# Identity, causal mask and row masks from GpSimd's affine selects in place of a load, and the second pair's output products ahead of the third FFN step

## The chip, the cores and the metric

The kernel runs on one NeuronCore of a Trainium2 chip. The metric is the device time of one execution in microseconds; the engines are TensorE (PE), VectorE (DVE), ScalarE (ACT), GpSimd (POOL) and SyncE (SP, which only issues DMAs here).

## The reference

A chunked state-space layer feeds a feed-forward layer with squared ReLU. Cut to what matters:

```python
# x (4, 8, 768, 32), a (4, 8, 768), B and C (4, 8, 768, 16), chunk 32
for c in range(nc):
    cum = np.cumsum(log_a[chunk], axis=-1)
    L = np.exp(cum[..., :, None] - cum[..., None, :]) * causal
    M = einsum('bhin,bhjn->bhij', Cc, Bc) * L
    y_intra = einsum('bhij,bhjd->bhid', M, xc)
    y_inter = einsum('bhin,bhnd->bhid', Cc, state) * exp(cum)[..., None]
    y[chunk] = y_intra + y_inter
    state = exp(sum(la)) * state + sum_j Bx * exp(cum[-1:] - cum)
t = y.transpose(0, 2, 1, 3).reshape(3072, 256)
h = maximum(t @ w_in, 0)          # w_in (256, 2048)
out = (h * h) @ w_out             # w_out (2048, 256)
```

## The kernel before

The kernel does not use the reference's chunk of 32. It cuts each of the 4 sequences of 768 tokens into 3 pieces of 256, and works on the 12 pairs (batch, piece) one after the other; `PAIRS` is piece-major, so the first four pairs have no state to carry in. A pair's 256 tokens are two halves `u` of 128, and each half is split by token parity `r`, so that 64 pairs of tokens lie on 64 partitions. The causal factor `exp(cum_i - cum_j)` is split into `P_i * (1/P_j)`, with `P` a running product of `a` (`cp_r`, by DVE's scan on line 484): C is multiplied by `P` and x by `1/P` (`Pinv`), and the products of C and B (`mt`, line 227) are then masked with 0 and 1 (`ph_mask`, line 238).

For one pair the stages are these. `ph_load` loads C, B and x on SP's queue; its `gate` argument is an engine that writes one element of each destination with a memset first, so that the load can't be issued before that engine has come so far. `prep_c`, `prep_b`, `prep_x` scale and cast. `ph_tr` (PE and a DVE copy) or, from pair 4 on, `ph_dtr` (a DMA) transpose. `ph_mt` makes `mt`, `ph_mask` makes `mts`; `ph_u` and `ph_s` make the state (`U`, `z`, `S`); `ph_y` makes the pair's output in PSUM. For pairs 1 to 3 `ph_y` does the products inside the half first (`y_intra`, line 314, 32 small matmuls of `xs` and `mts`), then those with the state (line 347, 8 matmuls of `bct` and `S`), and ends with ScalarE's copy `T` (line 366).

The FFN of one pair ("block") is 8 steps `fp`, two slices of 128 of the 2048 hidden units each. `mm1` is 4 matmuls into a PSUM tile `hps` (pool of 2 buffers), followed by ScalarE's ReLU into `hb` (line 381). `square` is DVE's `h2` (line 387). `mm2` is 4 matmuls into the block's output sum (line 405). `finish_block` copies and stores.

Everything stands under a manual schedule: the program order written in the Python code is the order in each engine's queue. The list `steps` gives the order of FFN steps: steps 0 to 3 are the first half of block 0, 4 to 7 that of block 1, 8 to 15 the second halves, then blocks 2 to 11. In step `s` the loop does: `mm1`, some warm-up matmuls in steps 1 and 2, then what `at(s, ...)` put into `todo`, then `square` of the step before, and from step 4 on one `mm2`. So block 0 runs while pair 1 is still being made: `ph_mt(1)` and two masks are in step 0, `ph_u(1)` and the other masks in step 1, and `ph_y(1)` is called ahead of `mm1` of step 3. Step 4 is the first that needs `T[1]`.

The weights come in four chunks each, cast from fp32 to bf16 on the way, on GpSimd's DMA queue (`load_wi`, line 136; `load_wo`, line 141). The first chunk of `w_in` is issued behind a one-element copy `touch` (line 499) that waits for `P_T`; the second behind `prep_x(0)`; two chunks of `w_out` follow, then `prep_x(1)`, then the memsets that gate the loads of pair 2, then the third chunk of `w_in`. The last three chunks wait behind a `touch` of `T[1]` (line 569, `late_loads`).

The constants come in two DMAs on ScalarE's queue: `cb` (bf16: the identity, the causal mask, `own`, which marks the row's block of 32, and `half`, which marks the row's 16 within it) and behind it `cf` (fp32: `pick` and `spread`, from which `sel` is made on line 481). ScalarE copies the identity and `half` out of `cb` as fp32 (lines 479 and 480). `sel` times `cp_r` gives `P_T` (line 496).

## Time and profile before

| What | Value |
|---|---|
| median of 11 runs | 119.97 us (118.44 to 122.27) |
| the profiled execution | 119.81 us |
| its span, from the first to the last instruction | 118.0 us |
| mean granted TensorE clock in it | 0.998 |
| PE busy | 110.4 us, 94% of the span, 1672 matmuls |
| DVE, ACT, POOL busy | 86.0, 76.3, 33.5 us |
| DMA | 13.63 MB, mean 115 GB/s |

The profile is of one execution. Its times count from the start of the span, and line numbers are those of the kernel before. PE is a matmul, PEld its weight load. In the tables "<-" after an idle time names what ended it; "issue" is idle time for which the profile shows no cause. A line of the chain is start, duration, what. A line of the stretch table is the stretch, its length, then busy us and number of instructions of PE, PEld, DVE, ACT and POOL, then the granted clock, the mean busy share of the 16 DMA engines and GB/s. A line of DMA queues is the queue, packets, MB, and the time that they took as a share of 16 engines' time.

### The profile page before, as it was taken

The numbers are of one execution on the slowest core, as the hardware profiler recorded it, in microseconds if no ns is written. First come the engines' busy times: TensorE is split into PE (matmuls) and PEld (weight loads), VectorE is DVE, ScalarE is ACT, GpSimd is POOL, SyncE is SP. The second block draws the span as 40 slices with busy tenths as digits, with TensorE's granted clock in tenths as the row PEclk, the third lists the DMA queues.
The fourth block names the chain that finished last, engine by engine and source line by source line (L and its number), as shares of the span: only waits on it lengthen the run. The fifth ranks groups of instructions, "written<-read, shape, count | busy, mean of one in ns | idle before, by whom it ended". The sixth has DMA issues, their size and how long they took to land.

```text
span 118.0 us, 4065 instructions
## 1 busy us (share of the span) xinstructions
PE 110.4 (94%) x1672; PEld 91.0 (77%) x1672; DVE 86.0 (73%) x204; ACT 76.3 (65%) x146; POOL 33.5 (28%) x69
## 2 busy tenths in 40 slices
PE   6799669999999999999999999999999999999970
PEld 4576448877977788788788887887887887888960
DVE  6479834699889699798698894984966967844530
ACT  4546738848678577586586677576775865867730
POOL 0079408604884350530404432504300000000000
PEclk9999999999999999999999999999999999999999
DMA  3999999999899945907908928549160020100202
GB/s 86 188 172 119 113 192 197 156 182 183 154 221 169 195 56 129 203 10 159 180 24 166 148 77 164 101 123 190 26 158 8 0 89 6 55 34 0 91 3 89
DMA packets 50019, 13.63 MB, mean 115 GB/s; under 512 B 44304, under 2 KB 49104, under 8 KB 50000
## 3 DMA queue, kind: packets, MB, share of 16 engines
q1 hardware_dynamic: 46400, 10.98, 50.6%
q0 software_dynamic: 3200, 2.10, 13.6%
q10 hardware_dynamic: 400, 0.28, 1.0%
q8 instruction: 13, 0.21, 0.8%
q14 instruction: 6, 0.05, 0.1%
HBM read 10.74 MB, written 3.15 MB: 118 GB/s over the span
## 4 chain that ended last, share of the span: by engine, by line
PE 85%; DMA 8%; ACT 1%; issue 1%; POOL 1%; DVE 0%; ACTq 0%; DVEq 0%
PE ops L405 35%; PE hps L377 35%; DMA w_in_b<-in_moe_w_in_dram 5%; PE Y L314 3%; PE mt L227 3%; DMA cf<-const_f 3%; PE Y L343 2%; PE U L256 1%; PE ctpt L496 1%; POOL xs L183 1%; PE ops_r L405 1%; PE ops L421 1%; PE ops_r L421 1%; PE Y L347 1%; ACT T L366 1%
## 5 line engine op out<-in xcount | busy, mean ns | idle before, releaser
L381 ACT ACTIVATE hb<-hps 128x512 bf16<-128x512 f32 x96 | 57.5, 599 | 30.0 <-PE hps L377 28.9
L377 PE MATMUL hps<-T,w_in_b 128*128 128x256 bf16 x384 | 57.6, 273 | 1.0 <-DMA w_in_b<-in_moe_w_in_dram 0.7
L405 PE MATMUL ops<-w_out_b,h 128*128 128x256 bf16 x360 | 55.0, 273 | 0.0
L387 DVE TENSOR_TENSOR h<-hb 128x512 bf16<-128x512 bf16 x96 | 40.7, 445 | 12.4 <-ACT hb L381 12.3
L377 PEld LDWEIGHTS <-w_in_b 128*128 128x128 bf16 x384 | 37.1, 98 | 5.8 <-DMA w_in_b<-in_moe_w_in_dram 1.2
L405 PEld LDWEIGHTS <-h 128*128 128x128 bf16 x376 | 34.5, 98 | 6.3 <-issue 2.0
L238 DVE TENSOR_TENSOR mts<-mt,cb 128x512 bf16<-128x512 f32 x44 | 29.1, 683 | 9.5 <-PE mt L227 9.4
L183 POOL TENSOR_TENSOR xs<-x_nat,Pinv 128x512 bf16<-128x512 f32 x12 | 13.3, 1108 | 10.2 <-DVE z L293 4.1
L152 POOL TENSOR_TENSOR bc<-C_nat,P_sb 128x128 bf16<-128x128 f32 x16 | 6.7, 441 | 23.4 <-DMA C_nat<-in_C_dram 19.3
L300 DVE TENSOR_TENSOR S<-z,Pown 128x256 bf16<-128x256 f32 x16 | 8.2, 514 | 0.5
L475 PE MATMUL dps<-dum 128*128 128x128 bf16 (+1 forms) x58 | 7.1, 274 | 1.1 <-DVE dum L457 1.1
L366 ACT CAST T<-Y 128x512 bf16<-128x512 f32 x11 | 6.4, 586 | 1.0 <-PE Y L347 1.0
L475 PEld LDWEIGHTS <-dum 128*128 128x128 bf16 x58 | 5.0, 116 | 2.5 <-DVE dum L457 1.1
L443 ACT COPY osb<-ops 128x512 f32<-128x512 f32 x11 | 6.4, 581 | 0.2 <-PE ops L405 0.2
L314 PE MATMUL Y<-mts,xs 64*32 64x128 bf16 x384 | 5.2, 219 | 0.7 <-issue 0.7
L227 PE MATMUL mt<-bct 32*64 32x256 bf16 x192 | 5.3, 291 | 0.0
L314 PEld LDWEIGHTS <-xs 64*32 64x32 bf16 x384 | 3.0, 91 | 2.3 <-issue 1.3
L177 POOL CAST bc<-B_nat 128x128 bf16<-128x128 f32 x16 | 4.5, 308 | 0.7 <-DMA B_nat<-in_B_dram 0.5
L227 PEld LDWEIGHTS <-bct 32*64 32x64 bf16 x192 | 1.9, 105 | 2.5 <-issue 1.7
L293 DVE SCALAR_TENSOR_TENSOR z<-z,Ptot,U 128x64 f32<-128x64 f32 x12 | 3.2, 266 | 0.5 <-PE U L256 0.3
L141 POOL DMA_DIRECT2D w_out_b<-in_moe_w_out_dram x4 | 3.1, 775 | 0.3 <-issue 0.3
L136 POOL DMA_DIRECT2D w_in_b<-in_moe_w_in_dram x4 | 3.1, 782 | 0.0
(72 smaller groups left out, 55.1 us busy)
## 6 DMA issues: line engine op xcount, KB each, us to landing
x_nat<-in_x_dram SPq DMA_DIRECT2D x12, 256.0 KB, 4.4
out_dram<-osb SPq DMA_DIRECT2D x7, 256.0 KB, 2.3
C_nat<-in_C_dram SPq DMA_DIRECT2D x12, 128.0 KB, 3.4
B_nat<-in_B_dram SPq DMA_DIRECT2D x12, 128.0 KB, 3.8
w_in_b<-in_moe_w_in_dram POOLq DMA_DIRECT2D x4, 256.0 KB, 6.2
w_out_b<-in_moe_w_out_dram POOLq DMA_DIRECT2D x4, 256.0 KB, 7.3
out_dram<-osb SPq DMA_DIRECT2D x8, 128.0 KB, 1.8
bct<-bc SPq DMA_TRANSPOSE x8, 4.3
```

The lines of the kernel that those rows point to most:

```text
L152: eng.tensor_tensor(out=_fap(bc[k % 3], r * 384 + 128, [[144, 2], [32, 4], [1, 16]]), in0=_fap(loaded[k]["C"], r * 16, [[128, 2], [32, 4], ...
L183: eng.tensor_tensor(out=_fap(xs, 0, [[256, 2], [32, 8], [1, 32]]), in0=_fap(loaded[k]["x"], 0, [[32, 2], [64, 8], [1, 32]]), in1=_fap(Pinv ...
L227: nc.tensor.matmul(mt[q // 2][64 * u:64 * u + 64, q % 2, r, :, :], bct[32 * q:32 * q + 32, r, 0, u * 64:u * 64 + 64], _fap(bct[32 * q:32 * ...
L238: nc.vector.tensor_tensor(out=v["mts"][:, q], in0=v["mt"][q // 2][:, q % 2] if src is None else src, in1=_fap(cb, 128, [[128, 2], [0, 2], ...
L300: nc.vector.tensor_tensor(out=S_n.rearrange("p (g q d) -> p g q d", g=2, q=4), in0=_fap(z, 0, [[32, 2], [0, 4], [1, 32]]), in1=_fap(Pown, ...
L314: nc.tensor.matmul(Y[u][32 * q:32 * q + 32, g, :], v["xs"][64 * u:64 * u + 64, r, h * 32:h * 32 + 32], v["mts"][64 * u:64 * u + 64, q, r, ...
L366: nc.scalar.copy(out=_fap(T[k], 0, [[64, 2], [128, 4], [1, 64]]), in_=_fap(Y[0], 0, [[512, 2], [64, 4], [1, 64]]))
L377: nc.tensor.matmul(hps[:, i, :], w_in_b[:, g, f * 128:(f + 1) * 128], T[blk][:, g].rearrange("p r u t -> p (r u t)"), start=(g == 0), stop ...
L381: nc.scalar.activation(out=hb, in_=hps, func=AF.Relu)
L387: nc.vector.tensor_tensor(out=h2, in0=hb, in1=hb, op=ALU.mult)
L405: nc.tensor.matmul(o[c], h2[:, i, r * 128:(r + 1) * 128], w_out_b[:, f, c * 128:(c + 1) * 128] if len(o) > 1 else w_out_b[:, f, :], start= ...
L475: nc.tensor.matmul(idle[-1][:, 0:cols], dum[:, 0:128], dum[:, 0:cols], start=True, stop=True, skip_group_check=True)
```

## The change

The DMA of `cb` is gone. `cb` is now made on the chip: DVE fills a tile `ones`, and GpSimd's `affine_select` keeps a one where an affine expression of partition and column fulfils a condition and writes zero elsewhere. The first makes the identity in fp32 (`eye_f`), from which ScalarE now copies the bf16 one (`eye_b`), the other way round than before. Two make an 8-wide `hq`, which DVE reduces to `half`. Two make the causal mask, one for each half of the partitions, and two make `own`. `cf` is loaded as before, and is now the first on ScalarE's queue.

Two things move in the order of work. `ph_y(1)` is called ahead of `mm1` of step 2 in place of step 3. The loads of pair 2, with their three gating memsets on GpSimd, move from ahead of step 0 into step 2, behind a one-element copy that waits for the last mask of pair 1 (`mts[:, 2]`).

```diff
-    cb = const.tile([128, 390], BF16, name="cb")
+    cb = const.tile([128, 388], BF16, name="cb")
...
+    ones = const.tile([128, 256], FP32, name="ones")
+    hq = const.tile([128, 2, 4], FP32, name="hq")
...
         nc.sync.dma_start(out=a_nat, in_=_dap(a, 0, [[256, 96], [1, 256]]))
-        nc.scalar.dma_start(out=cb, in_=cb_d.ap())
         nc.scalar.dma_start(out=cf, in_=cf_d.ap())
...
         nc.vector.memset(dum, 0.0)
+        nc.vector.memset(ones, 1.0)
+
+        def where(out, src, pattern, cm, base, op):
+            nc.gpsimd.affine_select(out=out, in_=src, pattern=pattern, compare_op=op, fill=0.0,
+                                    base=base, channel_multiplier=cm)
+
+        where(eye_f, ones[:, 0:128], [[-1, 128]], 1, 0, ALU.is_equal)
+        where(hq, ones[:, 0:8].rearrange("p (g q) -> p g q", g=2), [[-16, 2], [-32, 4]], 1, 0, ALU.is_ge)
+        where(hq, hq, [[16, 2], [32, 4]], -1, 15, ALU.is_ge)
+        for u in range(2):
+            where(_fap(cb[64 * u:64 * u + 64], 128, [[128, 2], [64, 2], [1, 64]]),
+                  _fap(ones[64 * u:64 * u + 64], 0, [[128, 2], [64, 2], [1, 64]]),
+                  [[-1, 2], [1, 2], [2, 64]], -2, 0, ALU.is_ge)
+        where(cb[:, 384:388], ones[:, 0:4], [[-32, 4]], 1, 0, ALU.is_ge)
+        where(cb[:, 384:388], cb[:, 384:388], [[32, 4]], -1, 31, ALU.is_ge)
         nc.vector.memset(zer, 0.0)
...
-        nc.scalar.copy(out=eye_f, in_=eye_b)
-        nc.scalar.copy(out=half, in_=cb[:, 388:390])
+        nc.scalar.copy(out=eye_b, in_=eye_f)
+        nc.vector.tensor_reduce(out=half, in_=hq, op=ALU.add, axis=mybir.AxisListType.X)
...
         recip(2, 2, 0)
-        ph_load(2, gate=nc.gpsimd)
         idle_tile()
...
         at(0, load_wi, 8, 12)
+
+        def third_loads():
+            nc.gpsimd.tensor_copy(out=touch, in_=live[1]["mts"][:, 2, 0, 0, 0:1])
+            ph_load(2, gate=nc.gpsimd)
+
+        at(2, third_loads)
...
         for s in range(len(steps) + LAG):
-            if s == 3:
+            if s == 2:
                 ph_y(1)
             if s < len(steps):
                 mm1(*steps[s])
```

## The prediction

> **What bounds the kernel now.** I read the page first, then the chain that ended last in its first 19 us, then the DMA queues by stretch, and last a table of instruction counts by stretch.

> ```profile
> PE   6799669999999999999999999999999999999970
> DMA  3999999999899945907908928549160020100202
> ```

> These are the page's slices of 2.95 us. TensorE is full from the seventh slice to the end; only the first six, about 18 us, have holes, and there DMA is full. From 18.36 us on no PE wait is listed. So whatever the change does to the head moves the end one for one, unless it opens a hole later. The chain in that head (start, us, what):

> ```profile
> 1.12 3.02 DMA cf<-const_f
> 4.15 0.02 issue
> 4.17 0.41 ACT sel L481
> ...
> 4.67 1.20 PE ctpt L496 x4
> ...
> 7.56 1.01 POOL xs L183
> 8.57 6.39 DMA w_in_b<-in_moe_w_in_dram
> ...
> 15.01 0.61 PE hps L377 x4
> ...
> 15.78 0.34 PE Y L314 x29
> 16.12 0.66 issue
> 16.78 0.23 PE Y L314 x3
> ...
> 17.29 0.59 ACT T L366
> ```

> Three things to see. The start hangs on cf (4.15) and on a_nat (a_cl at 3.77). The third FFN step waits for the second chunk of w_in_b (14.96). And in the middle of the second pair's output products PE stops for 0.66 us with nothing to wait for: 29 of 32 matmuls run, then "issue".

> The last one decides this forecast, so I looked for what it is. The page has a queue that carries nothing of the kernel's data, and the stretch table counts PE and PEld instructions:

> ```profile
> q8 instruction: 13, 0.21, 0.8%
> ```
> ```profile
> 10.27:16.50 6.23, 4.56 (x129) 3.09 (x128) 4.63 (x14) 3.46 (x8) 2.80 (x7) 1.00 1.06 127
> 16.50:27.34 10.84, 10.41 (x128) 8.27 (x128) 7.01 (x17) 7.23 (x16) 4.34 (x9) 1.00 1.24 182
> 27.34:36.10 8.76, 8.76 (x130) 7.05 (x127) 8.09 (x17) 6.43 (x13) 6.55 (x13) 1.00 1.11 186
> ```

> ```profile
> q0 software_dynamic: 452, 0.37, 86.2%
> ```
> ```profile
> q0 software_dynamic: 365, 0.19, 131.4%
> q8 instruction: 1, 0.02, 5.7%
> ```

> The first answer is for 10.3 to 14.2 us, the second for 14.2 to 15.3. In neither do SP's loads of the third pair appear, though they were issued at 12.03: they too stood behind GpSimd's weight chunks.

> [...] L183's 1108 ns for 512 elements is 2.2 ns each[...]; no run here shows a select.

> **The change part by part.** Times are of the profiled execution (119.81 us, 118.0 of span).

> *Constants.* Removed: cb's DMA (97.5 KB, landed 3.4), its issue of 0.36 us ahead of cf on ACT's queue, two ACT copies (0.30 and 0.19). cf is issued at 0.74 in place of 1.12 and should land near 3.3 to 3.8. Added on DVE: memset of ones, 256 elements; L462's take 0.79 us for two of 384, so 0.27. It delays the gate of x's first load from 2.42 to 2.69, and x's landing from 6.8 to 7.1; xs starts at 7.56, so 0.2 us of cover is left after the gain below. The small reduce (0.2, by L486's 0.18) stands ahead of a_cl, but DVE would be idle there for 0.89 - 0.27 us. Added on ACT: eye_b's copy (0.30) right behind the table load (ends 2.89), ahead of sel: done at 3.2 if the identity is.

> Added on GpSimd: seven selects from about 1.3 us. By L177 (308 ns for 128 elements) and L499 (189 ns for one) below and L152 (441) and L183 above: identity 0.3 to 0.45, two masks 0.45 to 0.65 each, four small ones 0.2 each: 2.0 to 2.6 us, done by 4.0. GpSimd is idle until 6.39 (wait of 5.9 us for P_T), so I take nothing. The cover ends if they take over 5 us.

> So the start hangs on a_nat. If that still lands at 3.75, the scans end at 4.84 as before, but the first matmuls of L496 run during the second scan: P_T 0.14 sooner. If it lands 0.3 sooner with cb out of the way, 0.42. I take 0.3; the first mm1, the masks and the chunks' issue all follow by that.

> The chunks' data don't follow wholly. Loads of the first two pairs (six of 1024 packets each) keep the DMA engines full to about 9 us, then the first two w_in chunks to 14.2. [...] What is saved is cb's own traffic (about 0.1) and the thin stretch at 10 to 11 us: 0.1 to 0.4, I take 0.25 for the second chunk, and so for the fetch behind it: PE's block is there at 16.78 - 0.25 = 16.53.

> *Order.* The program has the same instructions in PE's queue up to U of the second pair. Before, then come mm1 of step 2 (8 instructions), warm-up (6) and 59 of the products: boundary. After, the 64 of the intra part come first, then 9 of the inter part: the boundary falls with 4 of its 8 matmuls left. So PE reaches it sooner, near 15.0, and stands until 16.53. What follows, counted from the block's arrival a:
> - before: T's copy starts a + 0.51 (17.29), ends a + 1.10; mm1 of step 4 starts a + 1.14 (17.92), its psum slot long free, since step 2's ReLU ran at 15.65.
> - after: T's copy starts about a + 0.42, ends a + 1.01. Step 2's mm1 (0.44) is behind the boundary and runs beside it. Its ReLU is behind T on ACT: a + 1.61. With two hps buffers step 4 needs that slot: a + 1.66.

> So the order costs 0.52 while the fetch sets the time, less 0.25 for the earlier fetch: +0.27. The 0.74 us wait for w_in_b disappears, but is paid again at the boundary.

> *Third pair's loads.* Three memsets and three SP issues move from 11.91 behind the masks (14.72 - 0.3, plus 0.19 for the touch, as L569): C at about 14.75 in place of 12.03. No SP DMA is passed, as none stood between. On GpSimd they come behind the third w_in chunk, and Pown and the touch for the late chunks behind them; neither is late, T being later. In before these loads, issued at 12.03, moved nothing before 15.3 anyway; at 14.75 they stand behind w_out's second chunk, so from about 17.1. Between 18.5 and 20.5 GpSimd's queue is nearly empty (the next chunk is issued at 18.46, about 2 us before its data), and C and B fit there: B at 20.9 to 21.5 (before: 12.49 + 8.4 = 20.9). Its reader:

> ```profile
> 22.55 0.49 ACT L175 CAST Bb<-B_nat 128x128 bf16<-128x128 f32 x2
> ```

> Behind it on ACT stand the ReLUs, for which PE waits. Slack 1.9 us; x (22.1 before) is first used by U at 26.5. I take nothing; the bound is below, in the slower rival.

> Sum: 119.81 + 0.27 = 120.1. The median of 11 runs is 119.97, 0.16 above the profiled execution, so this says no change; a measurement of this kernel can tell about 1%, 1.2 us, from none.

> **Rivals.**
> *The fetch comes in time (30%).* The 6.5 us from 10.27 to 16.78 depend on where the fetch falls among the chunks. Early by 1.5 us, the products end near 15.0 and T near 15.7, step 2's ReLU at 16.35 and step 4 starts at 16.4: 1.5 us under 17.92. About 0.2 is given back, as everything reaches the third pair's B sooner: 118.5. For it: later crossings show no stop. Against: the chunks ahead of it stay.
> *The third pair's B is late (21%), slower.* It decides once B lands 1.9 us later than before, since ACT blocks on Bb and its ReLUs with it. If the landing moves with the issue by all of 2.7 us, the stall is 0.8; if T is early, the late chunks close the gap at 18.5 to 20.5 and x and the fourth pair (whose C is already waited for 4.8 us) follow, another 0.5 or more. 120.1 + 0.8 + 0.5 = 121.4.
> *The selects are slow (7%), slower.* [...] It begins to bite past 6.1 us. [...]

> **How the numbers follow.** Likeliest (42%): 120.1, by itself 119.3 to 121.0 (fetch 0.8 sooner, or not sooner at all with 0.4 of waits for B). From the rivals: faster by over 1% 0.22 (most of the first), slower 0.26 (all of the selects, most of late B, a little of the likeliest), within 1% 0.52. The range 118.4 to 121.4 takes in nearly all of the first rival and half of the second.

> **What would show it.** Right: PE's wait in the inter products (L338) of over 1 us put down to "issue", with the q8 transfer near 14; no wait of hps for w_in_b in step 2; ACT running T before the ReLU of step 2; GpSimd's selects done by 4; P_T copied at 5.5 to 5.8; Bb's cast without a wait. Wrong: no "issue" wait in the products, a DMA wait ahead of Bb or tr of the third pair, or a P_T later than 5.9.

## The result: no gain, about one per cent slower or the same

| | changed | before |
|---|---|---|
| first measurement, median of all executions (us) | 120.41 (119.06 to 123.08, 12) | 120.36 (117.95 to 123.84, 47) |
| ratio | 1.0096 [1.0057, 1.0134] | |
| measured again later, median (us) | 121.15 (119.09 to 124.38, 14) | 120.75 (117.56 to 124.31, 51) |
| ratio | 1.0007 [0.9946, 1.0069] | |
| profiled execution (us) | 121.76, span 120.1 | 119.81, span 118.0 |

Executions of one kernel mostly differ by up to 6%, partly by a stretch of 3.4 or 6.8 us in which TensorE runs at half speed, so the ratios compare only the executions near each kernel's fastest (most of them have no such stretch), and medians of all executions stand beside them.

The forecast was 120.1 us and no change. The time lies inside the range, but the first measurement puts the changed kernel 1% above the one before (the second leaves no difference), and the steps that were to lead to 120.1 were mostly not those that happened. What decided was the part of the change that the title does not name, the later loads of the third pair.

First the page's slices of the changed kernel, 3.0 us each:

```profile
PE   6896799938999999999999999999999999999990
PEclk9999999998699999999999999999999999999999
DMA  3999999999759971862933916909624020020202
```

Before, the last hole of PE lay in the sixth slice. Now the ninth slice has 3 tenths, and behind it the granted clock falls. The chain that ended last, in the first 32 us (start, us, what):

```profile
0.81 2.49 DMA a_nat<-in_a_dram
...
5.97 5.72 DMA w_in_b<-in_moe_w_in_dram
...
12.78 1.95 DVE mts L229 x4
...
15.18 0.25 PE Y L338 x8
...
15.45 0.59 ACT T L357
...
16.17 0.07 POOL touch L574
16.24 10.04 DMA x_nat<-in_x_dram
...
26.41 1.07 POOL xs L174
...
27.53 0.25 PE U L247 x16
```

The start hangs on `a_nat`, as forecast. The inter products run through (x8 in one piece), with no stop put down to "issue" (below, an issue stop). T starts at 15.45 in place of 17.29. Then comes what was not forecast: x of the third pair takes 10.04 us from its issue to its landing, and U (the state product of the third pair) waits for `xs`, the scaled x. (The chain puts x's issue behind `touch`. In the program it follows SP's issue of B, which ended at 16.15; the two only fall together.) Before, U started with no idle time ahead of it:

```profile
26.48 0.26 PE L256 MATMUL U<-xs,Bb 64*32 64x64 bf16 x16
```

PE's waits in the changed kernel from 10 to 34 us (in total, times, longest):

```profile
PE U L247 <- POOL xs L174: 2.3, 1, 2.3
PE hps L368 <- DMA w_in_b<-in_moe_w_in_dram: 1.1, 1, 1.1
```

And the stretch behind that wait, where the last but two figures is the granted clock:

```profile
27.50:33.00 5.50, 5.47 (x85) 3.86 (x85) 2.82 (x7) 2.58 (x6) 4.20 (x9) 0.69 0.91 167
```

From 28.9 to 32.3 us the clock records give one half.

The account of the profiled execution: the first `mm2` product starts at 17.06 instead of 18.36, -1.30 us; the wait for x +2.3; 3.4 us at half clock cost about 1.7 (an estimate, half of 3.4). That is +2.7. At the 961st PE record (the one that began the stretch at 36.10 before) the changed kernel is at 38.65, +2.54. At the issue of the last stores it is still +2.56 (117.06 in place of 114.50), at the end of the span +2.0: the last 0.5 came back behind that issue, after all matmuls. The second trace of the changed kernel (e9) shows the same kind of gain and loss without the half-clock stretch; of its other executions only times and clocks are known (4 of the first 12 had such a stretch).

### The profile page after: what moved, and what is told of

The parts are those of the page before. It is cut to its first block, busy times and chain, and to the rows that moved or that the text cites. A ratio compares the mean times of both kernels' runs of the same rounds, so it can differ in the third digit from the quotient of the medians.

```text
span 120.1 us, 4076 instructions
## 1 busy us (share of the span) xinstructions
PE 110.7 (92%) x1672; PEld 90.8 (76%) x1672; DVE 86.6 (72%) x206; ACT 76.3 (64%) x145; POOL 35.6 (30%) x77
## 4 chain that ended last, share of the span: by engine, by line
PE 77%; DMA 15%; DVE 3%; POOL 1%; issue 1%; ACT 0%; DVEq 0%; POOLq 0%
PE ops L396 32%; PE hps L368 31%; DMA x_nat<-in_x_dram 8%; DMA w_in_b<-in_moe_w_in_dram 5%; PE Y L305 3%; PE mt L218 3%; DMA a_nat<-in_a_dram 2%; DVE mts L229 2%; PE Y L334 1%; PE U L247 1%; PE ctpt L502 1%; POOL xs L174 1%; PE ops_r L396 1%; PE ops L412 1%; PE Y L338 1%; PE ops_r L412 1%
## 5 line engine op out<-in xcount | busy, mean ns | idle before, releaser
L368 PE MATMUL hps<-T,w_in_b 128*128 128x256 bf16 x384 | 58.4, 275 | 1.2 <-DMA w_in_b<-in_moe_w_in_dram 1.1
L396 PE MATMUL ops<-w_out_b,h 128*128 128x256 bf16 x360 | 55.6, 275 | 0.0
L378 DVE TENSOR_TENSOR h<-hb 128x512 bf16<-128x512 bf16 x96 | 41.7, 454 | 14.2 <-ACT hb L372 14.0
L368 PEld LDWEIGHTS <-w_in_b 128*128 128x128 bf16 x384 | 37.6, 99 | 6.2 <-DMA w_in_b<-in_moe_w_in_dram 1.3
L481 PE MATMUL dps<-dum 128*128 128x128 bf16 (+1 forms) x58 | 6.8, 264 | 1.1 <-DVE dum L447 1.1
L291 DVE TENSOR_TENSOR S<-z,Pown 128x256 bf16<-128x256 f32 x16 | 7.3, 459 | 0.5
L481 PEld LDWEIGHTS <-dum 128*128 128x128 bf16 x58 | 4.6, 110 | 2.4 <-DVE dum L447 1.1
L247 PE MATMUL U<-xs,Bb 64*32 64x64 bf16 x64 | 1.0, 195 | 2.7 <-POOL xs L174 2.3
L247 PEld LDWEIGHTS <-Bb 64*32 64x32 bf16 x64 | 0.6, 89 | 3.4 <-issue 2.5
```

The costliest lines, as they stand in the source:

```text
L291: nc.vector.tensor_tensor(out=S_n.rearrange("p (g q d) -> p g q d", g=2, q=4), in0=_fap(z, 0, [[32, 2], [0, 4], [1, 32]]), in1=_fap(Pown, ...
L368: nc.tensor.matmul(hps[:, i, :], w_in_b[:, g, f * 128:(f + 1) * 128], T[blk][:, g].rearrange("p r u t -> p (r u t)"), start=(g == 0), stop ...
L378: nc.vector.tensor_tensor(out=h2, in0=hb, in1=hb, op=ALU.mult)
L396: nc.tensor.matmul(o[c], h2[:, i, r * 128:(r + 1) * 128], w_out_b[:, f, c * 128:(c + 1) * 128] if len(o) > 1 else w_out_b[:, f, :], start= ...
L481: nc.tensor.matmul(idle[-1][:, 0:cols], dum[:, 0:128], dum[:, 0:cols], start=True, stop=True, skip_group_check=True)
```

## Experiments

All are edits of one of the two kernels. Medians are over all executions; `before` is its median on the same chip.

| run | what | median us (n) | before | ratio |
|---|---|---|---|---|
| e1_loads_back | changed, third pair's loads ahead of step 0 | 118.60 (14) | 120.02 | 0.9994 [0.9949, 1.0039] |
| e2_order_only | before, only the earlier `ph_y(1)` | 121.86 (22) | 120.02 | 1.0044 [0.9998, 1.0091] |
| e3_consts_only | before, only the constants | 119.41 (22) | 120.02 | 0.9974 [0.9936, 1.0013] |
| e4_loads_only | before, only the moved loads | 121.75 (6) | 120.02 | 1.0180 [1.0023, 1.0337] |
| e5_chunks_later | changed, late weight chunks later | 119.83 (22) | 120.00 | 1.0034 [0.9992, 1.0077] |
| e6_x_first | changed, third pair's x loaded first | 123.76 (6) | 120.00 | 1.0243 [1.0169, 1.0317] |
| e7_fewer_pe_instructions | before, 28 PE instructions fewer | 119.33 (14) | 120.00 | 1.0052 [1.0007, 1.0097] |
| e8_pe_kept_busy | changed, PE work ahead of U | 123.19 (6) | 120.00 | 1.0160 [1.0059, 1.0262] |
| e10_loads_back_fewer | e1 and 28 PE instructions fewer | 118.48 (6) | 120.75 | 0.9885 [0.9823, 0.9946] |
| e11_changed_fewer | changed, 28 PE instructions fewer | 120.60 (22) | 120.75 | 1.0117 [1.0076, 1.0158] |
| e12_chunks_later_fewer | e5 and 28 PE instructions fewer | 119.72 (22) | 120.75 | 0.9999 [0.9949, 1.0049] |
| e13_changed_fewer_busy | e11 and PE work ahead of U | 120.63 (6) | 120.04 | 1.0120 [1.0049, 1.0191] |
| e14_loads_back_fewer_2 | e10 once more | 119.10 (22) | 120.04 | 0.9974 [0.9938, 1.0010] |

### The change taken apart

**e1_loads_back**: the changed kernel without `third_loads`.

```diff
         recip(2, 2, 0)
+        ph_load(2, gate=nc.gpsimd)
...
-        at(2, third_loads)
```

> The changed kernel with the third pair's loads back where they were, ahead of step 0; selects and the new order stay. Theory A (the late x of the third pair eats the gain): x lands near 22 in place of 26.3, no wait of U for xs, no stretch at half clock near 29 to 32, the 1.3 us won by 17 us stays: ratio to before 0.985 to 0.992. Theory B (selects or order cost by themselves): still 1.00 or above. Theory C (the loads' early issue holds up the second w_in chunk or the instruction fetch): an issue wait in the products is back, ratio near 1.00.

118.60 us: 1.8 under the changed kernel's first median and 1.4 under before by medians; the ratio to before, 0.9994, says no change, so the expected 0.985 to 0.992 was missed. In its profile (117.41 us) U starts at 24.59 with no wait for x, which lands at 22.3; the clock stays full. So constants and order are not the loss, and the moved loads are the suspect; e4 and, on one chip, e10 and e11 ask that more directly.

**e2_order_only**: before, with `if s == 2: ph_y(1)` and nothing else.

> The kernel before with the products of the second pair ahead of the third FFN step, nothing else. By the prediction's step (instruction block late, near 16.8) the products stand at the block boundary, first output matmul of step 4 about 0.5 us later than before, ratio 1.003 to 1.005. If the block comes early, a wait of U for w_in goes and the ratio is 0.990 to 0.995.

```profile
PE Y L347 <- issue: 0.4, 1, 0.4
```

The stop falls into the inter products with 4 of their 8 matmuls left, as the prediction placed it, and x is in time (U at 26.57, no wait). 121.86 us against 120.02, but 13 of its 22 executions have a mean clock under 0.99, against 12 of 51 before; the ratio, +0.4%, has no change just inside its interval. Taken alone the order is no gain.

**e3_consts_only**: before, with the constants made by selects and nothing else.

> The kernel before with the constants made by selects and nothing else. Theory A: P_T near 5.4 (0.5 sooner), instruction block asked for 1 us sooner and there by 15, no issue wait in the products; third pair's loads in time: first output matmul about 0.9 us sooner, ratio 0.990 to 0.996. If the selects cost: ratio 1.00 or above.

```profile
PE Y L305 <- issue: 1.9, 1, 1.9
```

119.41 us, a ratio that leaves anything from -0.6 to +0.1%. The profiled execution (123.0 us) was an unlucky one: the block came late, PE stood 1.9 us in the intra products (to 17.80), and 6.8 us at half clock began within that stop, at 17.16. It shows that the issue stop is not a fixed cost: it is 0.66 us in the profile of before, 0.4 in e2, 1.9 here and none in the changed kernel.

**e4_loads_only**: before, with `third_loads` and nothing else.

> The kernel before with the third pair's loads behind the masks of the second pair and nothing else. Theory A says that the loads are late only because the late weight chunks follow at once: here T is at 17.9 as before, chunks issued 18.5, so x lands at 22 to 24 and U waits for at most 0.3 us: ratio 0.998 to 1.004. If the move alone is enough to make x late: x at 26 or later, U waits 1 to 2 us and a stretch at half clock follows, ratio 1.02 or more.

```profile
PE U L256 <- POOL xs L183: 2.0, 1, 2.0
```

1.8% slower, from six executions and with a wide interval. The first expectation, T late as in the kernel before and x in time, did not come about: in this trace T starts at 15.49. The wait for x is there without the rest of the change, and again 3.4 us at half clock follow (from 28.1). With e1 this shows which part loses the time.

### Why x is late

The three loads of the changed kernel are issued at 15.15 (C), 15.62 (B) and 16.24 (x) and the three late weight chunks at 16.62, 17.42 and 18.11. C and B land after 4.7 and 4.9 us, x after 10.04. From 18.5 us to 22.4 the chunks move 0.31 MB before and 0.51 MB in the changed kernel (in this order):

```profile
q0 software_dynamic: 561, 0.31, 64.5%
q1 hardware_dynamic: 2064, 0.39, 53.1%
```
```profile
q0 software_dynamic: 785, 0.51, 98.2%
q1 hardware_dynamic: 1016, 0.13, 22.2%
```

(q0 is GpSimd's queue with the chunks, q1 SP's.) SP's loads moved 0.39 MB in this stretch before and 0.13 MB in the changed kernel. Three experiments ask whether these chunks are what x stands behind.

**e6_x_first**: the order x, C, B.

```diff
-            ph_load(2, gate=nc.gpsimd)
+            ph_load(2, "xCB", gate=nc.gpsimd)
```

> The changed kernel with the order of the third pair's three loads changed: x, C, B in place of C, B, x. Theory (only the last of the three falls behind the late chunks): x lands by 22, U does not wait for xs; B, now last but half as large, lands near 23 to 25, so that ACT's cast of it and the ReLUs behind it wait up to 2 us, PE standing for less than that. Rival (the late start alone counts, any of the loads takes 8 to 10 us): x lands near 25 and U waits as before. Time: 119 to 121 by the theory, 120.4 or more by the rival.

```profile
PE tr L199 <- ACT Bb L166: 3.0, 1, 3.0
```

x lands at 19.5 and U does not wait. B, now last, lands at 24.7, ACT's cast of it (`Bb`) waits, and PE stands 3.0 us at the transposes, with 3.4 us at half clock behind. 2.4% slower, and all six executions have a mean clock under 0.99. That is above the theory's 119 to 121; the rival's "120.4 or more" takes in the time, but not the trace, where U does not wait. In both orders the last of the three loads is late and the first two are in time.

**e5_chunks_later**: the chunks gated on a later product.

```diff
-            nc.gpsimd.tensor_copy(out=touch, in_=T[1][:, 0, 0, 0, 0:1])
+            nc.gpsimd.tensor_copy(out=touch, in_=h2s[(1, 0)][:, 0, 0:1])
...
-        at(5, late_loads)
+        at(6, late_loads)
```

> The changed kernel with only the three late weight chunks moved: they are issued behind the first square of the second block (as late as in the kernel before, near 18.4 us) instead of behind T of the second pair (16.6). Theory (x of the third pair stands behind these chunks): x lands near 22 to 23.5 instead of 26.2, U's wait for xs falls from 2.3 us to under 0.5, the half-clock stretch after it goes away, and the median comes to about 118.5, 1% or more under the changed kernel. Rival (x is late because its own issue came 1.6 us later, whatever stands around it): x lands at 25 or later, U still waits over 1.5 us, 120 or more. If the chunks come too late themselves, mm1 of w_in's fourth part or the second product of step 12 waits for DMA.

Its one profile answers half of the question. PE's block came only at 19.3 (fetch at 17.0), PE stood 3.5 us, and the chunks were issued at 24.3, so U's need for x was not put to the test. But x, issued at 16.66, later than in the changed kernel, landed at 22.92, 6.3 us on: against the rival, its late issue alone does not make it late. 119.83 us is below the changed kernel's two medians, in the expected direction, short of the expected 118.5. To ask again with T early in each execution, I first had to move the block boundary.

**e7_fewer_pe_instructions**: before, with warm-up matmuls of twice the width and half the number.

```diff
-        warm(14, 128)
+        warm(7, 256)
...
-        warm(8, 128)
+        warm(4, 256)
...
-            warm(6, 128)
+            warm(3, 256)
```

> The kernel before with 28 idle warm-up matmuls of 128 columns replaced by 14 of 256: 28 PE instructions fewer ahead of the second pair's output products, at the same PE time. Theory (the 0.66 us issue stop in those products is the 256-instruction block boundary waiting for its fetch): the stop moves 28 instructions later in the program, behind the products, into the first products of the third and fourth FFN steps; the products run through, T comes about 0.5 us sooner, time 0 to 0.5 us less. Rival (the stop belongs to that place, whatever the number of instructions): it stays after 29 of the 32 products.

PE's timeline (start, us, what, and the idle time before with its releaser):

```profile
15.18 0.42 PE L314 MATMUL Y<-mts,xs 64*32 64x128 bf16 x32
...
15.75 0.50 PE L377 MATMUL hps<-T,w_in_b 128*128 128x256 bf16 x3
17.49 0.71 PE L377 MATMUL hps<-T,w_in_b 128*128 128x256 bf16 x5 [1.23 <-issue]
```

The products run through, and the stop moves into the first FFN products behind them, 28 instructions on: it belongs to the count of instructions, not to the place. It is no smaller (1.2 us, the fetch at 15.2). The expected 0 to 0.5 us less is not shown: the median is 0.7 us lower, but the ratio is half a per cent higher, and no change lies outside its interval. T is now free of the boundary.

**e10_loads_back_fewer, e11_changed_fewer, e12_chunks_later_fewer**: the same edit of the warm-up put into e1, into the changed kernel and into e5. They ran on one chip, together with the changed kernel itself (**e9_changed_again**, second measurement in the first table).

> The changed kernel itself once more, beside the next three on one chip, to have more of its executions and a second trace. Theory: x of the third pair is the last of three loads that start only 1 to 2 us ahead of the late weight chunks, so an execution whose instruction block comes in time (T of the second pair at about 16) has x at 25 to 26 and U waiting about 2 us, and one whose block comes late (T at 17 or later, chunks later too) has x in time: both come to 119.5 to 120.5, or to about 122 where a half-clock stretch follows. Rival: the first trace was one unlucky execution, and the median is 118.5.

> The changed kernel with the third pair's loads back ahead of step 0 (118.6 before) and 28 idle PE instructions fewer ahead of the products (14 warm-up matmuls of 256 columns for 28 of 128), so that PE's block boundary falls behind the second pair's products, into the products of the third FFN step. Theory: T no longer waits for a late block, the rest of a stop is paid one time in w_in's products; x in time; median 118.0 to 118.6, hardly any execution with a half-clock stretch. Rival (the block was no longer limiting in that kernel): the same as without, 118.6.

> The changed kernel with 28 idle PE instructions fewer ahead of the products, and nothing else. Theory: T of the second pair now comes early in every execution, so the late weight chunks are issued about 1 us behind x's load every time, x lands at 25 or later, U waits about 2 us: what the head gains is given back, 119.5 or more by median, and 1% or more above the same kernel with the loads back ahead of step 0. Rival (the head's gain stays): 118.5 or less, within 0.3% of that kernel.

> The changed kernel with 28 idle PE instructions fewer, and the three late weight chunks issued behind the first square of the second block instead of behind T, about 1.5 to 2 us later. Theory (x stands behind these chunks): x lands at 22 to 23.5, U waits under 0.5 us, median 118.0 to 119.0, 1% under the same kernel with the chunks behind T. Rival (the loads' own late issue counts): x at 25 or later and no gain. A third way: the chunks now stand in the way of the third and fourth pair's loads or come late themselves, which a wait of a second product (w_out) or of the fourth pair's transposes for a DMA would show.

The changed kernel had no unlucky first trace: in its second one (119.28 us) U waits 1.8 us for xs, without a half-clock stretch behind. (9 of its 14 executions have a mean clock under 0.99.) e11 waits longest, 2.7 us, and its chain is that of the changed kernel:

```profile
15.92 0.07 POOL touch L574
16.00 10.15 DMA x_nat<-in_x_dram
```

With the chunks later (e12: the first issued 2.7 us behind x's load, at 17.74 and 15.02, in place of 0.4 us in e11, at 16.38 and 16.00) x lands 5.6 us after its issue, and GpSimd's timeline has xs without any wait:

```profile
20.79 1.06 POOL L174 TENSOR_TENSOR xs<-x_nat,Pinv 128x512 bf16<-128x512 f32 x1
```

against 26.29 in e11. In e12 x was also issued 1 us sooner than in e11. That this is not the cause is seen in e4, where x was issued at 15.09, as in e12, but the first chunk at 16.66 in place of 17.74:

```profile
15.09 10.38 DMA x_nat<-in_x_dram
```

It landed at 25.47 there, at 20.66 in e12. What x stands behind are the chunks. By time: 120.60 with the chunks behind T, 119.72 with the chunks later, 118.48 with the loads early; ratios 1.0117, 0.9999 and 0.9885. The first interval lies clear of the other two; the last clears the middle one by a hair, from six executions. The 119.72 of e12 is above the expected 118.0 to 119.0. In its trace the third way of the expectation shows: PE waits 0.5 us at 24.47 for a w_in chunk, which the later issue has made late. **e14_loads_back_fewer_2** repeats the last with more executions:

> The kernel with the loads back ahead of step 0 and 28 idle PE instructions fewer once more, as it had only 6 executions (118.48 us): the median stays at 118.0 to 118.8, 1% or more below the kernel before, with few half-clock stretches; U does not wait for xs. Rival: the 6 were lucky ones, and the median comes to 119.5 or more.

119.10, above the expected 118.0 to 118.8, ratio 0.9974 with no change still inside its interval, U without a wait for xs. Two of its 22 executions took 216 us; I have no explanation, and the first six had none. So the best version of this study is the change without its moved loads (118.60, 118.48 and 119.10 in three measurements); by the ratios to the kernel before, 0.9994, 0.9885 and 0.9974 against 1.0096, 1.0007 and 1.0117 of the versions with them, it is about 1% under the changed kernel and 0 to 1% under the kernel before.

### The half clock behind the wait

**e8_pe_kept_busy**: the changed kernel with idle matmuls in front of U.

```diff
             U = [t[:, u, 0:64] for u in range(2)]
+            if k == 2:
+                for _ in range(36):
+                    nc.tensor.matmul(t[:, 0, 256:384], dum[:, 0:128], dum[:, 0:128],
+                                     start=True, stop=True, skip_group_check=True)
```

> The changed kernel with 36 matmuls of 128x128 on constant data, into unused columns of U's accumulator, ahead of U of the third pair: about 1.9 to 2.0 us of PE work in the place where PE waits for xs. Theory (idle time of about 2 us makes TensorE run at half speed for the next 3.4 us): U starts at the same time, 27.5, but no half-clock stretch follows, mean clock 0.995 or more, and the time is about 1.5 us under the changed kernel: 118.9. Rival (the clock falls for other reasons and at other times): the stretch stays, and the time stays at 120.4 or above.

Inconclusive: in the profiled execution x was in time (landed at 23.5, U reached after 27.7), the half-clock stretch lay elsewhere (16.8 to 20.2), and the 36 matmuls were pure cost. But the stretch tells against the theory as the only cause: in the 3.41 us ahead of it PE has no gap over 0.55 us and is busy 59%. **e13_changed_fewer_busy** puts 44 of them into e11, where x was late in the one trace.

> The changed kernel with 28 idle PE instructions fewer (120.6 us, where U of the third pair waits 2.7 us for xs and 6 of 22 executions have a half-clock stretch), and in addition 44 matmuls of 128x128 on constant data ahead of that U: about 2.3 us of PE work where PE would stand. Theory (PE standing about 2 us or more makes a half-clock stretch likely): U starts as late as without them, the wait for xs shrinks to 0.5 us or less, no execution or hardly one has a clock of 0.986, and the slowest executions (above 121.5) are gone; the median is 120.0 to 120.6. Rival (the stretches are not due to that idle time): as many executions at 0.986 as without, and the median the same or, where x isn't late, up to 2 us more.

```profile
25.94 2.63 PE L244 MATMUL U<-dum 128*128 128x128 bf16 x44
28.50 0.25 PE L251 MATMUL U<-xs,Bb 64*32 64x64 bf16 x16
```

Here xs is done at 28.34, late again, but PE does not stand, and 0 of 6 executions have a half-clock stretch, against 6 of 22 in e11; at e11's rate, six without one have a chance of 0.15, so this speaks for the theory and doesn't prove it. The median did not move (120.63 against 120.60; 120.0 to 120.6 was expected). Nor is the stretch a mark of late loads: the kernel before, with x in time in its trace, has a mean clock under 0.99 in 55 of the 164 executions measured beside these runs, e11 in 6 of 22.

## Why the prediction was wrong

- **The start**: right up to P_T. cf out of the way, `a_nat` sets it. P_T is copied at 5.36 instead of 5.90: 0.54 sooner, forecast 0.3. But the text went on "the first mm1, the masks and the chunks' issue all follow by that", and only the issue did: the first w_in chunk, issued at 5.97 in place of 6.51, landed at 11.69 in place of 11.70, and the first mm1 starts at 11.74 in both. Before:

```profile
11.74 0.61 PE L377 MATMUL hps<-T,w_in_b 128*128 128x256 bf16 x4
```

  The second chunk, forecast 0.25 sooner, landed at 15.02 in place of 14.96. So in these two traces the 1.3 us of the head come from the products that no longer stand behind that chunk and from the stop that is gone, not from an earlier start of the FFN.
- **The selects**: right that they cost nothing. The identity takes 0.29 us (forecast 0.3 to 0.45), a mask 0.42 (0.45 to 0.65), the small ones 0.19, and all are done by 3.5 (forecast 4.0). A mask's 421 ns for 256 columns is 1.6 ns each. The third rival, the slow selects, had no measurement behind it and did not come about. The groups of the selects, with their busy time, mean ns of one, and the idle time before them:

```profile
L451 POOL TENSOR_SCALAR_AFFINE_SELECT cb<-ones 64x256 bf16<-64x256 f32 x2 | 0.8, 421 | 0.1
L451 POOL TENSOR_SCALAR_AFFINE_SELECT eye_f<-ones 128x128 f32<-128x128 f32 x1 | 0.3, 292 | 0.9 <-DVE ones L448 0.9
```

- **The fetch**: wrong, and in the hopeful direction. The term "0.25 sooner" measured 2.2: q8 starts at 12.03 in place of 14.22, and no issue stop is left. In this execution the first rival (30%) happened, as far as the head goes. I had counted only what the DMA queue does and not when PE comes to the end of its first block; in all 16 traces the first fetch lies behind that end, by 2.1 to 6.3 us. (That the end of a block sets off the fetch is my reading of this and not tested.) The end came at 9.21 in place of 10.27; the other 1.1 us of the 2.2 is a shorter way from that end to the fetch (2.82 in place of 3.95), for which I have no cause. Of the 1.06 only about half is the earlier P_T. The rest is TensorE's clock. From PE's timeline of before, then of the changed kernel (start, us, what):

```profile
5.66 0.63 PE L502 MATMUL ctpt<-eye_f,C_r 128*128 128x128 f32 x2
7.01 0.71 PE L475 MATMUL dps<-dum 128*128 128x128 bf16 x5
```
```profile
5.16 0.38 PE L508 MATMUL ctpt<-eye_f,C_r 128*128 128x128 f32 x2
6.23 0.44 PE L481 MATMUL dps<-dum 128*128 128x128 bf16 x5
```

  The same matmuls take 0.6 times as long. The clock records say full speed from 8.4 us on before, from 5.0 on in the changed kernel; the page's PEclk shows 9 ahead of that in both, so it does not tell. In the six traces with a half-clock stretch it lasts 3.41 or 6.83 us, and the first stretch at full speed in the changed kernel lasts 23.89, 7 times 3.41.

  In nine of the 16 profiles here full speed came at 3.8 to 5.8 us (block's end 8.95 to 9.68, fetch at 11.5 to 13.3), in seven at 8.4 to 10.4 (block's end 10.27 to 11.34, fetch at 13.2 to 17.0). What decides between the two is not shown. PE's idle time ahead of its first products with `cp_r` (L496, in the changed kernel L502) is 0.65 us before and 0.17 in the changed kernel, but with 0.27 in e2 full speed came late, and with 0.39 in e4 early. Nor is it shown that the new constants help: full speed came late in 3 of the 4 traces with the old ones and in 4 of the 12 with the new.

  With a fetch that starts anywhere between 11.5 and 17.0, the "likeliest" case was one draw among several, and I had taken the profile of before for the rule.
- **The order**: the working was right where its condition held: e2 has its stop with 4 of 8 left. In the changed kernel the block was there, and nothing was to be paid.
- **The third pair's loads**: here the time went, and this is the step that failed. C and B were right: C is issued at 15.15 (forecast 14.75), B lands at 20.5 (20.9 to 21.5), and Bb's cast has no wait. But for x the text said "first used by U at 26.5. I take nothing". It rested on a lull of the chunks from 18.5 to 20.5, read from a trace in which T was late. The chunks are gated on T. With T at 15.45 they were issued from 16.62, not 18.46; there was no lull; and the last of the three loads, which is also the largest, stood behind them until 26.3, while U wanted xs at 25.2. The term "nothing" was a wait of 2.3 us. The slower rival named that ("if T is early, the late chunks close the gap", "x ... follow") but put the loss on B and ACT, at 0.8 us, and x at "another 0.5". Measured: x alone, 1.8 to 2.7 us of PE's time, and B nothing.
- **The price of a stop**: missing. A wait for x was followed by 3.4 us at half speed in two of the four profiles in which PE waits for xs and nothing is put in its place (the changed kernel, 2.3 us, and e4, 2.0), about 1.7 us more (an estimate, half of 3.4). In these two the clock fell behind gaps of 2.3 and 2.0 us, with PE busy 41% of the 3.41 us ahead of the fall, and in e8 it fell with no gap over 0.55 in the 3.41 us ahead.
- **The sum**: 120.1 came out near 120.41 by luck, since two wrong terms had opposite signs: -1.3 in the head, where +0.27 was forecast, and +2 to +4 at x, where nothing was.

What stays open: what decides which wait is followed by the half clock. The second trace of the changed kernel and e11 have 3.41 us around the wait (24.58 to 27.99, 25.68 to 29.09) in which PE was busy 46% and 43%, and no stretch followed; the six traces with a stretch have 35 to 59% in the 3.41 us ahead of it. So neither the length of a gap nor the busy share by itself tells them apart.

## What to carry to other kernels

A load that is moved later is judged by the transfers issued just behind it as well as by its own slack: write down what gates those, and work it out for the case that the rest of the change succeeds, since an early T here pulled 768 KB of weights onto the late load. Try the parts of a change alone: here two of the three together cost nothing, and the third ate what they gave. And ask of an earlier issue what it moves: the first chunk, issued 0.54 us sooner here, landed at the same time. And read from the length of the first matmuls (here 0.63 us or 0.38 for the same two), not from the clock row, at which speed TensorE starts.

## What was not expected of the hardware

- The place of PE's stop for instructions followed the count: 28 instructions fewer ahead of it moved it by as many (e7). It lasted 0 to 3.5 us between the traces of this case, with 2.1 to 6.3 us from the end of the first block to the first q8 transfer. That its length hangs on when the block before ends and on the loads in the queues fits the traces, but no run tests it by itself.
- SP's loads did not keep their pace beside GpSimd's chunks: 256 KB of x took 10.04, 10.15 and 10.38 us from issue to landing in the changed kernel, e11 and e4, with three chunks issued within 3.1 us behind them, and 5.6 us in e12, with the first of them 2.7 us behind. The distance to the chunks is not the whole rule: in e14, with x issued early (12.11) and the first chunk 3.4 us behind, it took 10.5 us, and in e8, with the first 1.1 us behind, 6.75. What counted for U was the landing, 22.6 in e14, in time.
- In these 16 traces TensorE came to full speed at 3.8 to 5.8 or at 8.4 to 10.4 us, and the end of PE's first block at 8.95 to 9.68 or at 10.27 to 11.34.
